# Attention with beacon keys, then a SwiGLU block: the hand-written order of the first quarter and of its loads written anew

## The chip, the cores and the metric

The kernel runs on one core of a Trainium2 chip. The metric is the device time of one execution in microseconds. A core has TensorE (PE, matrix products), VectorE (DVE), ScalarE (ACT), GpSimd (POOL), SyncE (SP, here only an issuer of DMAs) and 16 DMA engines; each engine works through its own instructions in order, and semaphores tie them together.

## What is computed

Attention over 8 batches of 8 heads, 576 tokens and head size 64, with 16 extra "beacon" keys in front that every token sees; then a gated feed-forward block on the 4608 tokens.

```python
k_all = np.concatenate([beacon_k, k], axis=2)
v_all = np.concatenate([beacon_v, v], axis=2)
scores = scale * np.matmul(q, k_all.transpose(0, 1, 3, 2))
scores = np.where(causal, -1000000000.0, scores)      # beacon columns are never masked
a = np.exp(scores - scores.max(-1, keepdims=True))
a /= a.sum(-1, keepdims=True) + 1e-09
x = np.matmul(a, v_all).transpose(0, 2, 1, 3).reshape(4608, 512)
g = x @ w_gate                                         # 512 -> 1536
return (g / (1 + np.exp(-g)) * (x @ w_val)) @ w_out    # 1536 -> 512
```

## The kernel before

All inputs come in as float32 and are turned into bfloat16 on the way, by DMAs that GpSimd issues (`rows`, `runs`, `w_load`, `load_wo`). A load takes one of eight DMA semaphores in turn, so the issue of a load waits for the landing of the load eight places earlier, and everything behind it on GpSimd waits too.

The work of one batch goes in four pairs of heads. Keys and queries have to be turned (head size onto the partitions). For batches 0 to 2 TensorE does that: `turn` (letter T in the plan below) writes `t_ps` in PSUM, and `turned_copy` brings it to `kT` and `qT`, on VectorE (K, Q) or on ScalarE (k, q). For batches 1 and 2 a pair's rows are first put side by side in SBUF by `pair_up`, on VectorE (g) or on GpSimd (f; 128x1152 elements into `side`). Later batches are turned by DMAs (t). The scores of a pair come in four units A to D (`scores`, S, or s where TensorE also adds the causal mask with two small products); `exponent` (E) is ScalarE's exp into `p`; `mask` sets masked elements to zero, on VectorE (D, a product with `ramp`) or on GpSimd (M, an affine select). `pv` (P and p, the two heads of a pair) multiplies with the values, `normalize` (R) on VectorE divides. The result is turned into `xT`, for batch 0 by TensorE (J, X), from batch 1 on by DMAs (V).

The feed-forward block goes over chunks of 512 tokens and 12 tiles of 128 hidden columns: `gate_value` (G, H; `gv_ps`) needs `wg` and `wv`, then tanh on ScalarE (a) and two products on VectorE (1, 2) give `hT`, and `project` (F; `o_ps`) multiplies with `wo`. Chunk 0 is cut: hidden tiles 0 to 5 are done for 240 tokens (units 0 to 5), then for 272 (units 6 to 11), then tiles 6 to 11 for all 512. The weights of `wg` and `wv` come in five parts each (g0 to g4, u0 to u4; parts 0, 1 and 2 hold hidden tile 0, tiles 1 and 2, and tiles 3 to 5), `wo` in two (o0, o1). K1, Q1, K2, Q2 are the keys and queries of batches 1 and 2, K0.0, Q0.0, K0.4, Q0.4 the later part of batch 0's for heads 0 to 3 and 4 to 7, v0.0 to v0.5 the beacon rows and five pieces of the values of batch 0, b1 and b2 beacon keys.

What every engine does, and in which order, is written out by hand: the string `plan` has one letter for each step, read from front to end, and each engine gets its steps in that order. Loads stand in the plan as L (free) or l (issued only after TensorE has done the step two before), and `order_of_loads` names which load each of them is. PSUM is cut into four slots of two banks (`take`, `give`): a step that takes a slot waits, on TensorE, for the step that gave that slot back. A letter h orders a filler, a product of 256 columns whose result nobody reads; it is put out at the next step that takes a slot for scores or values, and it writes into that slot:

```python
def keep_warm(ps):
    while heat:
        heat.pop()
        wide = ident[:, None, :].to_broadcast([P, 2, P])
        nc.tensor.matmul(ps[:, 0, 0 : 2 * P], lhsT=ident[:], rhs=wide, start=True, stop=True)
```

Of the kernel before, what the change touches and what calls it, by code (L numbers as in the profile page):

```python
# [84 lines left out]
def kernel(  # L85
# [731 lines left out]
    plan = """
    0LhbTqLLhhWKehTQsLTLEKLsqLkELhhSLTcQsKELKEsLssQEshsEhDELshEEELLhLTQZkNZsNSPpJEEILsJPLLERIpSXLDRP
    pSyEGXRHELDSyLDGaELGH1H2aaXD1Lf2Py1pGGLH2GRaXHlylH12aaGGH112a2HG1G2Haa1HaTq2lgGl1H2k1GaS21l2HSEa
    lsElGS12ETHgKQGEaS12lEHlTDa1GSqH2glDkESfaGslE1H2ElSEMDlTGMSQaKEHSMM12aGEs1HEa2T1qPpMllkDPfllSpRE  # L820
    2sRfsPDpSEEFEFFSFRDFFlSElSPEMpTFFlFERkFSfFFlqDSSFFFlEDFDEFSFTEFDFFFSQVlEkEFFDDFFOSEOllFFTtFqKFDl
    MSFESFFFFElSSMDlFElPplPlpERsFDFRFFFEFStlFFEGSGHtFDHDEaGMF1FFaH12POlOpaPp2RlG1GlRHtal2G1HHGVa21ll
    l2ltGHal1G2lGHHa1aatlt21tGH1H2lattF2aGFH112FF2FFGSaEFlHt1GFFaHa2Gltl1t2GtlH12latH12Fa12FFGGtDHSl
    tlaE1FHFFaG2lSFHtl12allF12GFElMFllFHaSG1FEFHaGFFolMHl2l1G2aSOF1H2FaE1FtFG2sHFEaFslF1FDFlSE2FDFED
    FSESlPpFFFRlDFFFlStFESSDFFEFFsEDFOPEpMPEOpSFFlFRMStRFEFEFSsFEMEFFDFFPplFSFFFFFlFRDSSEFEtFtSFDFFF
    FFEEFlVFFsoOElFFSFtFFDFtSMPEDEtSFElpSDRFFMFFtlMPtESSFEEpRFttFFGFDDSEGHFGa12HHlla1aG21FHl2aGlFHl1
    a2GSHD1ool2aDtPlEGM1ltp2HRlla1GtlSlGH2alEGHG1l2FaM1HHF2a1GFa2HS1FF2FSFFaEFSFEF12lFSPEFpDMFEFSlSR
    FFlEFFtSFttEFFDFSFVFFESEtFFFMsMDEFFFDFEsOFSFFolPttDEFDFSpFFEMFsESFRFFFEFFtFPMEGGOtHoSEtaplHRPtla
    11Gpt2HD2tGMRaGSt1HH2tGEa1al2G1HSa2GEH1a2GttHGa12SHH1a2MEG1GaM2DSHHES12FaEFFFFF1FDla2FFPSF1FE2Fp
    RFFSFFSEFSFESFFFFVEFSFFFFDDFEFFEFFDSoFPFFMlFpFEStlFERFFFFFSSDoEPMFFEFFFDDOMGpoRSElPHGa1S2pHEaR1G  # L830
    2sHlGGEDaHaD12GG1Ha2H12aG1Ha2HaGG12S1EHlHGa2a1D2MSH1FEl2GSMFa1H2EMPaFDF1FSF2EDFFFpSFEFFsRFFFSFFF
    SEFPEEFFSFpERFFSFFFMDVFMSFFDEEPFFDSoFFFFpFFFFEFDOFSPRFDFSpEGFFFEGRGDDFHaO1oHH2aa12P1GpRHGGH2VaGH
    a1a12HG2Ga1H122HGa1Ga2G1HHH2aa1a21G21GH2aG12HaHGFFFF1a2FFGF1H2aHaGF1H2FaF1GF2F1GHHFFFaa2FF12G1GH
    aFFFFH12F2FFFFFFaG1FHFFoFaFoFF212GGFHaFF1FHFF2FFaFGFFFFOHoG12GHHFaa12GFaFFF1FFF21FHF2GGFFaHFaFF1
    FFF12FHa2FG1GFHF2HFaF1FoaFFoFFFFFG2FF1FFHFaF1FGFF2HGFFFaFF12FH2FFaFFFFF1FFFFF2oFFFFFFFFFFFFOFFFF
    FFFOFoFFFFFFFFFFFOoFFFFFFOo
    """
# [42 lines left out]
```

## Time and profile before

| | us |
|---|---|
| median of 3 runs | 363.26 (363.25 to 364.06) |
| the profiled execution | 364.0 |
| its span in the trace | 362.0 |
| TensorE busy in the span | 353.9 (98%) |
| VectorE, ScalarE, GpSimd busy | 223.6, 189.0, 123.8 |
| mean granted share of TensorE's clock | 0.995 |

The span begins with the first instruction of the core and ends with the last one; 2.0 us of the profiled execution lie around it. Times in rows of the trace count from the start of the span. A row of the timeline merges equal instructions that follow each other ("x6"); in brackets behind a row stand the idle time of its engine just before it and what ended that. A matmul's row is longer than the distance to the next one, since matmuls overlap in the array.

### The profile page before, as it was taken

Reading aid. Unit: us, or ns where it says so; the run is one execution under the profiler, and the core shown is the slowest. Engines: PE = TensorE matmul, PEld = TensorE weight load, DVE = VectorE, ACT = ScalarE, POOL = GpSimd, SP = SyncE. Lnnn points to the kernel's source line nnn. Section 1 sums busy time; section 2 is a strip of 40 time slices with the busy share of each in tenths; the row PEclk is TensorE's granted clock in tenths of the full one; section 3 lists DMA queues with packets and bytes.
Section 4 is the critical chain, followed back from the end, with each engine's and each line's share of the span. In section 5 each row is a group of like instructions: output and inputs, shape, how many; then the busy total and the mean of one; then the engine's idle time right before and its main releaser. Section 6 shows DMA issues by size and latency. Waiting matters only on the chain.

```text
span 362.0 us, 11854 instructions
## 1 busy us (share of the span) xinstructions
PE 353.9 (98%) x5150; PEld 200.7 (55%) x5150; DVE 223.6 (62%) x437; ACT 189.0 (52%) x286; POOL 123.8 (34%) x185
## 2 busy tenths in 40 slices
PE   7899999999999999999999999999999999999996
PEld 4677566654444566544565556545655554455554
DVE  5577987667766753497518763777467764464341
ACT  4966989822425677543864466546633332331311
POOL 8935489936337544375423013112000000000000
PEclk9899999999999999999999999999999999999999
DMA  8999999999999999999999829602422000110113
GB/s 120 166 204 203 186 194 139 173 176 155 140 153 113 133 137 119 161 115 170 139 120 170 111 28 138 95 0 20 107 78 67 2 2 0 61 58 3 61 60 116
DMA packets 146132, 39.74 MB, mean 110 GB/s; under 512 B 131488, under 2 KB 141728, under 8 KB 146080
## 3 DMA queue, kind: packets, MB, share of 16 engines
q0 software_dynamic: 97424, 19.00, 73.4%
q1 hardware_dynamic: 48368, 19.76, 26.3%
q8 instruction: 40, 0.66, 0.8%
q10 hardware_dynamic: 288, 0.23, 0.2%
q14 instruction: 12, 0.10, 0.1%
HBM read 38.27 MB, written 9.44 MB: 132 GB/s over the span
## 4 chain that ended last, share of the span: by engine, by line
PE 84%; DMA 8%; POOL 4%; issue 3%; ACT 1%; POOLq 0%
PE gv_ps L173 46%; PE o_ps L173 26%; PE s_ps L173 5%; DMA wv<-in_moe_w_val_dram 4%; PE pv_ps L173 4%; PE pv_ps L505 3%; DMA wg<-in_moe_w_gate_dram 2%; DMA qk<-in_q_dram 2%; POOL qk L215 1%; POOL vb L225 1%; ACT p L414 0%; POOL wv L254 0%; POOL p L427 0%; POOL wo L258 0%; PE t_ps L171 0%
## 5 line engine op out<-in xcount | busy, mean ns | idle before, releaser
L173 PE MATMUL gv_ps<-xT,wv 64*128 64x512 bf16 (+2 forms) x912 | 203.2, 365 | 0.6 <-DMA wv<-in_moe_w_val_dram 0.6
L173 PE MATMUL gv_ps<-xT,wg 64*128 64x512 bf16 (+2 forms) x912 | 203.0, 365 | 0.1
L591 ACT ACTIVATE th<-gv_ps 128x512 f32<-128x512 f32 (+2 forms) x114 | 65.4, 575 | 118.0 <-PE gv_ps L173 117.6
L414 ACT ACTIVATE p<-s_ps 128x832 bf16<-128x832 f32 (+2 forms) x127 | 104.6, 869 | 34.4 <-PE s_ps L173 28.7
L173 PE MATMUL o_ps<-wo,hT 64*128 64x512 bf16 (+2 forms) x912 | 116.0, 365 | 0.4 <-ACT p L414 0.4
L596 DVE SCALAR_TENSOR_TENSOR u<-th,gv_ps 128x512 f32<-128x512 f32 (+2 forms) x114 | 74.7, 656 | 66.4 <-ACT th L591 65.7
L173 PEld LDWEIGHTS <-wg 64*128 64x128 bf16 x912 | 82.4, 94 | 45.7 <-PE gv_ps L173 2.4
L173 PEld LDWEIGHTS <-wv 64*128 64x128 bf16 x912 | 81.7, 94 | 40.7 <-DMA wv<-in_moe_w_val_dram 0.7
L603 DVE SCALAR_TENSOR_TENSOR hT<-gv_ps,u 128x512 bf16<-128x512 f32 (+2 forms) x114 | 74.7, 661 | 3.0
L173 PEld LDWEIGHTS <-hT 64*128 64x128 bf16 x912 | 43.4, 94 | 32.8 <-DVE hT L603 0.7
L225 POOL DMA_DIRECT2D vb<-in_v_dram x40 | 33.9, 851 | 63.0 <-PE s_ps L173 25.3
L173 PE MATMUL s_ps<-qT,kT 64*128 64x336 bf16 (+3 forms) x512 | 43.5, 254 | 1.4 <-ACT kT L262 0.8
L173 PEld LDWEIGHTS <-kT 64*128 64x128 bf16 x512 | 23.8, 94 | 22.6 <-issue 1.4
L423 DVE TENSOR_TENSOR p<-p,ramp 128x256 bf16<-128x256 bf16 (+2 forms) x84 | 23.9, 315 | 10.0 <-ACT p L414 9.8
L225 POOL DMA_DIRECT2D qk<-in_q_dram x25 | 21.2, 851 | 25.5 <-DMA qT<-qk 5.8
L534 DVE TENSOR_TENSOR x<-pv_ps,rec 128x640 bf16<-128x640 f32 (+1 forms) x32 | 25.3, 791 | 1.2
L533 DVE RECIPROCAL rec<-pv_ps 128x10 f32<-128x10 f32 (+1 forms) x32 | 6.8, 213 | 28.8 <-PE pv_ps L173 22.8
L225 POOL DMA_DIRECT2D qk<-in_k_dram x25 | 21.2, 851 | 5.7 <-PE gv_ps L173 4.4
L427 POOL TENSOR_SCALAR_AFFINE_SELECT p<-p 128x256 bf16<-128x256 bf16 (+2 forms) x46 | 17.5, 402 | 13.6 <-ACT p L414 13.3
L263 DVE COPY o_sb<-o_ps 128x512 f32<-128x512 f32 (+2 forms) x18 | 11.6, 657 | 16.5 <-PE o_ps L173 16.5
L173 PEld LDWEIGHTS <-p 64*128 64x128 bf16 x960 | 18.7, 94 | 4.5 <-PE pv_ps L173 0.2
L173 PE MATMUL pv_ps<-vb,p 64*128 64x65 bf16 x960 | 19.9, 189 | 0.0
(63 smaller groups left out, 142.8 us busy)
## 6 DMA issues: line engine op xcount, KB each, us to landing
out_dram<-o_sb SPq DMA_DIRECT2D x34, 256.0 KB, 3.6
vb<-in_v_dram POOLq DMA_DIRECT2D x24, 128.0 KB, 5.8
...
```

What stands on the lines that cost most here:

```text
L173: ins = nc.tensor.matmul(o, lhsT=l, rhs=r, start=start, stop=stop)
L225: return nc.gpsimd.dma_start(dst[p0 : p0 + n, c, :, 0:D], src[b, :, r : r + n, :].rearrange("h j d -> j h d"))
L263: return eng.tensor_copy(o, i)
L414: nc.scalar.activation(p_of(b, m, u == "A")[:, :, c0 : c0 + w], ps[:, :, 0:w], ACT.Exp, scale=0.125)
L423: nc.vector.tensor_tensor(out=ap, in0=ap, in1=upper[:, None, d : d + w].to_broadcast([P, 2, w]), op=ALU.mult)
L427: nc.gpsimd.affine_select(out=ap, in_=ap, compare_op=ALU.is_ge, fill=0.0, base=d, pattern=[[0, 2], [1, w]], channel_multiplier=-1,)
L505: ins = nc.tensor.matmul(o_ps[:, side, 68 * c : 68 * c + D + 1], lhsT=pt[n % NPT][:, side, col : col + P], rhs=vb[b % 2][:, t, 2 * m + sid ...
L533: nc.vector.reciprocal(rec[:, :, c0:NKT], o[:, :, :, D : D + 1])
L534: nc.vector.tensor_tensor(out=xs[b][:, c0:NKT, P * m : P * m + P].rearrange("p c (h d) -> p h c d", d=D), in0=o[:, :, :, 0:D], in1=rec[:, ...
L591: nc.scalar.activation(th[:, 0:w], gvs[n][:, 0, 0:w], ACT.Tanh, scale=0.5)
L596: nc.vector.scalar_tensor_tensor(out=u[:, 0:w], in0=ths[n][:, 0:w], scalar=1.0, in1=gvs[n][:, 0, 0:w], op0=ALU.add, op1=ALU.mult)
L603: nc.vector.scalar_tensor_tensor(out=hTs[j][:, f, c0:c1], in0=gvs.pop(n)[:, 1, 0 : c1 - c0], scalar=0.5, in1=ths.pop(n)[:, 0 : c1 - c0], o ...
```

## The change

Only the two strings are edited. In `plan`, the first 448 letters become 466; the 1307 letters behind them are the same. Up to that place each step occurs as often as before; what differs is the order, the engine of some steps, and the fillers:

| step, up to the common part | before | after |
|---|---|---|
| fillers (h) | 10 | 28 |
| masks on VectorE (D) / on GpSimd (M) | 22 / 9 | 10 / 21 |
| pairs put side by side on VectorE (g) / on GpSimd (f) | 3 / 5 | 0 / 8 |
| key copies on VectorE (K) / on ScalarE (k) | 7 / 6 | 6 / 7 |
| query copies on VectorE (Q) / on ScalarE (q) | 7 / 7 | 11 / 3 |
| batch 0's beacon copy | ScalarE (e) | VectorE (A) |
| later copies of `xT` (y / Y), of the output (O / o) | 4 / 0, 2 / 0 | 2 / 2, 1 / 1 |

The plan's second line shows how the values' steps of batch 0's pair 3 stand to unit 3 of the feed-forward block (the fourth G): before `...Py1pGG...` (P, p, then G3 and G4), now `...hPGap12a12G...` (P, G3, p, G4). The place where the common part begins is `POlOpaPp2RlG1G`, the values of batch 2, pairs 2 and 3.

The core of the diff:

```diff
     order_of_loads = """
-    K0.0 Q0.0 v0.2 Q0.4 K0.4 v0.1 v0.0 v0.3 v0.4 v0.5 g1 u0 g0 u1 g2 u2 K1 Q1 b1 u3 g3 g4 u4 Q2 v1.5 K2 v1.3
-    v1.2 v1.0 v1.1 v1.4 b2 o0 o1 v2.2 k3.0 v2.1 q3.2 v2.5 k3.5 v2.4 v2.3 v2.0 q3.4 q3.0 q4.2 k4.0 v3.3 k3.1 q4.0
+    Q0.0 K0.0 v0.0 K0.4 Q0.4 v0.2 v0.4 v0.1 v0.3 v0.5 u0 g1 g0 u1 u2 g2 K1 Q1 b1 u3 g3 b2 g4 u4 v1.0 Q2 K2 v1.1
+    v1.5 v1.3 v1.4 v1.2 o0 o1 q3.0 v2.2 q3.2 v2.1 v2.3 v2.0 v2.4 v2.5 k3.1 k3.5 k3.0 q3.4 k3.2 v3.3 q4.0 k4.2
...
     plan = """
-    0LhbTqLLhhWKehTQsLTLEKLsqLkELhhSLTcQsKELKEsLssQEshsEhDELshEEELLhLTQZkNZsNSPpJEEILsJPLLERIpSXLDRP
+    0TqTbQkLLWkAhhhshhhsTEQkhhhShsLETQEDLLkhhsLhsLLLLELETKLhsEQLELshhhsQhhhZEhhsKscEZNSEPNELLpEsPLpR
...
```

On ScalarE at the start, batch 0's copies out of `t_ps` (`qT_105`, `kT_107`) stand between the exps of the first units (`p_109`, `p_110`, `p_111` are the three buffers of `p`):

```order
 L262 ACTIVATE qT_105<-t_ps 128x256
-L262 ACTIVATE kT_107<-t_ps 128x4x16
-L414 ACTIVATE p_109<-s_ps 128x2x368
-L262 ACTIVATE qT_105<-t_ps 128x2x256
+L262 ACTIVATE kT_107<-t_ps 128x256 x2
+L414 ACTIVATE p_109<-s_ps 128x2x368
 L262 ACTIVATE kT_107<-t_ps 128x2x256
 L414 ACTIVATE p_110<-s_ps 128x2x368
 L414 ACTIVATE p_111<-s_ps 128x2x368
+L262 ACTIVATE kT_107<-t_ps 128x320
```

Three early key copies have come to ScalarE, the wide query copy and the beacon copy have left it.

Nine exps further on, still on ScalarE, the last key copy of batch 0 stood in the row of exps:

```order
 L414 ACTIVATE p_110<-s_ps 128x2x464
 L414 ACTIVATE p_110<-s_ps 128x2x416
-L262 ACTIVATE kT_107<-t_ps 128x2x320
 L414 ACTIVATE p_111<-s_ps 128x2x416
 L414 ACTIVATE p_111<-s_ps 128x2x464
```

It is now on VectorE, and the nine exps from batch 0's unit B of pair 0 on follow each other.

On GpSimd before, around the loads of `wo`: `qk_102` and `vb_103` are loads for batches 3 and 2, `side` is a pair of batch 2, the affine selects are masks of batch 1:

```order
L248 DMA beacons_100<-in_beacon_k_dram 16x8x64
L258 DMA wo<-in_moe_w_out_dram 128x6x512 x2
L263 COPY side<-qk_101 128x1152
L225 DMA vb_103<-in_v_dram 128x8x64
L225 DMA qk_102<-in_beacon_k_dram 16x8x64
L427 AFFINE_SELECT p_110<-p_110 128x2x128
L225 DMA vb_103<-in_v_dram 112x8x64
L427 AFFINE_SELECT p_111<-p_111 128x2x80
L427 AFFINE_SELECT p_111<-p_111 128x2x128
L427 AFFINE_SELECT p_109<-p_109 128x2x112
```

The same place now:

```order
L258 DMA wo<-in_moe_w_out_dram 128x6x512
L427 AFFINE_SELECT p_110<-p_110 128x2x112
L427 AFFINE_SELECT p_110<-p_110 128x2x128
L263 COPY side<-qk_102 128x1152
L427 AFFINE_SELECT p_110<-p_110 128x2x128
L427 AFFINE_SELECT p_111<-p_111 128x2x112
L427 AFFINE_SELECT p_111<-p_111 128x2x128
L258 DMA wo<-in_moe_w_out_dram 128x6x512
L263 COPY side<-qk_101 128x1152
L225 DMA qk_102<-in_q_dram 128x8x64
L225 DMA vb_103<-in_v_dram 128x8x64
L427 AFFINE_SELECT p_111<-p_111 128x2x128
```

Masks of batch 1, pairs 0 and 1, have moved ahead of the second load of `wo` and of batch 2's first pair; the beacon load b2 has left this place for one behind g3.

## Rows read from the trace of the kernel before

**Rows 1.** The page: busy time by engine.
```profile
PE 353.9 (98%) x5150; PEld 200.7 (55%) x5150; DVE 223.6 (62%) x437; ACT 189.0 (52%) x286; POOL 123.8 (34%) x185
```

**Rows 2.** Windows of 4 us: busy PE, PEld, DVE, ACT, POOL; clock, DMA, GB/s.
```profile
12.00:16.00 4.00, 4.00 (x98) 2.86 (x93) 1.16 (x4) 4.00 (x6) 3.40 (x6) 0.63 2.04 160
...
28.00:32.00 4.00, 4.00 (x71) 3.41 (x73) 3.18 (x9) 1.99 (x6) 0.37 (x1) 1.00 1.32 201
```

**Rows 3.** Timeline of ScalarE, batch 0: start, length, what.
```profile
11.47 4.81 ACT L414 ACTIVATE p<-s_ps 128x832 bf16<-128x832 f32 x6
16.11 0.77 ACT L262 ACTIVATE kT<-t_ps 128x640 bf16<-128x640 bf16 x1
17.23 2.46 ACT L414 ACTIVATE p<-s_ps 128x832 bf16<-128x832 f32 x3 [0.35 <-PE s_ps L173]
```

**Rows 4.** The chain of waits, 12 to 58 us: start, length, what.
```profile
15.16 7.66 DMA wg<-in_moe_w_gate_dram
...
23.11 15.64 DMA wv<-in_moe_w_val_dram
```

**Rows 5.** Timeline of TensorE around the fourth unit of the feed-forward block.
```profile
24.53 0.89 PE L505 MATMUL pv_ps<-vb,p 128*128 128x65 bf16 x24
25.37 0.26 PE L173 MATMUL gv_ps<-xT,wg 64*128 64x240 bf16 x1
26.18 0.27 PE L173 MATMUL gv_ps<-xT,wv 64*128 64x240 bf16 x1 [0.56 <-DMA wv<-in_moe_w_val_dram]
```

**Rows 6.** Timeline of TensorE, fillers of the start.
```profile
5.96 0.61 PE L187 MATMUL s_ps<-ident 128*128 128x256 bf16 x4
...
7.95 0.39 PE L187 MATMUL s_ps<-ident 128*128 128x256 bf16 x2
```

**Rows 7.** Timeline of TensorE behind that place, to the common part.
```profile
33.56 0.63 PE L173 MATMUL gv_ps<-xT,wg 64*128 64x272 bf16 x2
...
35.55 0.83 PE L173 MATMUL s_ps<-qT,kT 64*128 64x336 bf16 x8
...
49.92 1.47 PE L505 MATMUL pv_ps<-vb,p 128*128 128x65 bf16 x39
51.78 0.35 PE L505 MATMUL pv_ps<-vb,p 128*128 128x65 bf16 x6 [0.39 <-POOL p L427]
...
55.38 0.82 PE L173 MATMUL o_ps<-wo,hT 64*128 64x512 bf16 x6 [0.38 <-ACT p L414]
...
57.32 1.08 PE L505 MATMUL pv_ps<-vb,p 128*128 128x65 bf16 x30
...
78.00 1.99 PE L505 MATMUL pv_ps<-vb,p 128*128 128x65 bf16 x60
```

**Rows 8.** Timeline of GpSimd.
```profile
13.66 0.74 POOL L254 DMA_DIRECT2D wg<-in_moe_w_gate_dram  x1 [0.24 <-DMA qk<-in_k_dram]
...
46.40 0.82 POOL L258 DMA_DIRECT2D wo<-in_moe_w_out_dram  x1 [2.29 <-DMA qk<-in_k_dram]
47.22 1.16 POOL L263 COPY side<-qk 128x1152 bf16<-128x1152 bf16 x1
...
50.91 1.78 POOL L427 TENSOR_SCALAR_AFFINE_SELECT p<-p 128x160 bf16<-128x160 bf16 x5
```

**Rows 9.** Timeline of VectorE: a mask alone, and one while GpSimd copies (third row, GpSimd).
```profile
40.61 0.47 DVE L423 TENSOR_TENSOR p<-p,ramp 128x224 bf16<-128x224 bf16 x2
...
53.99 1.75 DVE L423 TENSOR_TENSOR p<-p,ramp 128x224 bf16<-128x224 bf16 x2
...
54.24 1.16 POOL L263 COPY side<-qk 128x1152 bf16<-128x1152 bf16 x1
```

**Rows 10.** Groups of instructions by shape, 0 to 80 us: count, busy us, mean ns.
```profile
L534 DVE TENSOR_TENSOR x<-pv_ps,rec 128x640 bf16<-128x640 f32 x7 | 5.8, 824 | 0.2
L603 DVE SCALAR_TENSOR_TENSOR hT<-gv_ps,u 128x512 bf16<-128x512 f32 x8 | 5.5, 688 | 0.2
...
L263 DVE COPY kT<-t_ps 128x576 bf16<-128x576 bf16 x3 | 2.2, 750 | 0.0
```

More of the change, by code (lines that the diff above doesn't have):

```diff
@@ L734 @@
     order_of_loads = """
-    K0.0 Q0.0 v0.2 Q0.4 K0.4 v0.1 v0.0 v0.3 v0.4 v0.5 g1 u0 g0 u1 g2 u2 K1 Q1 b1 u3 g3 g4 u4 Q2 v1.5 K2 v1.3
-    v1.2 v1.0 v1.1 v1.4 b2 o0 o1 v2.2 k3.0 v2.1 q3.2 v2.5 k3.5 v2.4 v2.3 v2.0 q3.4 q3.0 q4.2 k4.0 v3.3 k3.1 q4.0
-    k3.4 k3.2 q3.1 v3.0 k4.2 q3.3 k4.3 v3.5 q4.4 k3.3 v3.4 v3.2 k4.5 k4.1 q4.3 q4.1 v4.1 v4.5 v4.3 v4.0 k4.4
+    Q0.0 K0.0 v0.0 K0.4 Q0.4 v0.2 v0.4 v0.1 v0.3 v0.5 u0 g1 g0 u1 u2 g2 K1 Q1 b1 u3 g3 b2 g4 u4 v1.0 Q2 K2 v1.1
+    v1.5 v1.3 v1.4 v1.2 o0 o1 q3.0 v2.2 q3.2 v2.1 v2.3 v2.0 v2.4 v2.5 k3.1 k3.5 k3.0 q3.4 k3.2 v3.3 q4.0 k4.2
+    q4.2 k4.0 q3.1 q3.3 v3.0 k3.4 k4.3 v3.5 q4.4 k3.3 v3.4 v3.2 k4.5 k4.1 q4.3 q4.1 v4.1 v4.5 v4.3 v4.0 k4.4
     v3.1 v4.2 q6.1 k5.0 q5.1 q5.4 k5.3 k5.5 k6.0 k5.2 k5.1 q5.0 k6.2 q5.3 v4.4 k6.1 q6.0 q6.2 k6.5 q5.2 v5.2
@@ L817 @@
     plan = """
-    0LhbTqLLhhWKehTQsLTLEKLsqLkELhhSLTcQsKELKEsLssQEshsEhDELshEEELLhLTQZkNZsNSPpJEEILsJPLLERIpSXLDRP
[L819 to L836, printed above, removed]
+    0TqTbQkLLWkAhhhshhhsTEQkhhhShsLETQEDLLkhhsLhsLLLLELETKLhsEQLELshhhsQhhhZEhhsKscEZNSEPNELLpEsPLpR
+    SXEJyRIJIMPXEYpLRhShSLLLlEGGDHEGMXHLa1YHM2hPGap12a12GRHGLXla1yHf2aHaL1212lGGHHfGaa1G1l2HaHGa2T1H
@@ new lines @@
+    2Qlk1Gl2al1SEfHlhhhST2aGEsk1Q2EHla1SMGSEHE2STDQGEKSaH1sEfaM2MGlDfESHE12a1SGllE2MSHEaTsGqK1T2MHEP
+    QSpDkllMsaEP12ERsEpSRfPSlDpEESMFFFfTFRFElSllKqPSEpFMSFEFFFESlERFFTfVFFMlQkSSMEEFFFMMSEMFFFFFFFFF
+    DMTSlFOlotFEQlKFFFFSFESPpESMFFMEllRFPplRDsltlFEDlFSFFFESEDGMGHaFFFFHFGlF1ltM2Fla1HPOlOpaPp2RlG1G
+    lRHtal2G1HHGVa21lll2ltGHal1G2lGHHa1aatlt21tGH1H2lattF2aGFH112FF2FFGSaEFlHt1GFFaHa2Gltl1t2GtlH12l
+    atH12Fa12FFGGtDHSltlaE1FHFFaG2lSFHtl12allF12GFElMFllFHaSG1FEFHaGFFolMHl2l1G2aSOF1H2FaE1FtFG2sHFE
@@ new lines @@
+    aFslF1FDFlSE2FDFEDFSESlPpFFFRlDFFFlStFESSDFFEFFsEDFOPEpMPEOpSFFlFRMStRFEFEFSsFEMEFFDFFPplFSFFFFF
+    lFRDSSEFEtFtSFDFFFFFEEFlVFFsoOElFFSFtFFDFtSMPEDEtSFElpSDRFFMFFtlMPtESSFEEpRFttFFGFDDSEGHFGa12HHl
+    la1aG21FHl2aGlFHl1a2GSHD1ool2aDtPlEGM1ltp2HRlla1GtlSlGH2alEGHG1l2FaM1HHF2a1GFa2HS1FF2FSFFaEFSFEF
+    12lFSPEFpDMFEFSlSRFFlEFFtSFttEFFDFSFVFFESEtFFFMsMDEFFFDFEsOFSFFolPttDEFDFSpFFEMFsESFRFFFEFFtFPME
+    GGOtHoSEtaplHRPtla11Gpt2HD2tGMRaGSt1HH2tGEa1al2G1HSa2GEH1a2GttHGa12SHH1a2MEG1GaM2DSHHES12FaEFFFF
@@ new lines @@
+    F1FDla2FFPSF1FE2FpRFFSFFSEFSFESFFFFVEFSFFFFDDFEFFEFFDSoFPFFMlFpFEStlFERFFFFFSSDoEPMFFEFFFDDOMGpo
+    RSElPHGa1S2pHEaR1G2sHlGGEDaHaD12GG1Ha2H12aG1Ha2HaGG12S1EHlHGa2a1D2MSH1FEl2GSMFa1H2EMPaFDF1FSF2ED
+    FFFpSFEFFsRFFFSFFFSEFPEEFFSFpERFFSFFFMDVFMSFFDEEPFFDSoFFFFpFFFFEFDOFSPRFDFSpEGFFFEGRGDDFHaO1oHH2
+    aa12P1GpRHGGH2VaGHa1a12HG2Ga1H122HGa1Ga2G1HHH2aa1a21G21GH2aG12HaHGFFFF1a2FFGF1H2aHaGF1H2FaF1GF2F
+    1GHHFFFaa2FF12G1GHaFFFFH12F2FFFFFFaG1FHFFoFaFoFF212GGFHaFF1FHFF2FFaFGFFFFOHoG12GHHFaa12GFaFFF1FF
@@ L837 @@
+    F21FHF2GGFFaHFaFF1FFF12FHa2FG1GFHF2HFaF1FoaFFoFFFFFG2FF1FFHFaF1FGFF2HGFFFaFF12FH2FFaFFFFF1FFFFF2
+    oFFFFFFFFFFFFOFFFFFFFOFoFFFFFFFFFFFOoFFFFFFOo
     """
```

## Prediction

> **What bounds the kernel now.** The page comes first: TensorE is busy 98% of the span, no other engine over 62% [rows 1]. An edit that leaves TensorE's products alone can only take away time in which it waits, and all 8 us of idle time are spread over the span. Both strings change nothing behind the place where the common part of the plan begins, which TensorE reaches at 78.00 [rows 7]. So the question is when it gets there.
>
> Next come the windows and the timelines of the first 78 us. There are three stretches. **The first, to about 20 us, is ScalarE's**: from 11.47 its exps follow each other without a gap, six in 4.81 us (0.80 each), then a key copy of 0.77, a wait of 0.35, three more exps [rows 3], and the window from 12 to 16 shows it busy for 4.00 of 4.00 us [rows 2]. TensorE's clock stands at 0.63 in that window, so partly at the lower level, behind a stretch in which it had little to do; ScalarE sets the pace there, so it costs little.
>
> **The second ends at a landing.** At 25.37 TensorE begins the fourth unit of the feed-forward block (G3), the first that reads the third weight parts g2 and u2, and stands until 26.18 for the DMA of `wv` [rows 5]. This DMA isn't late because it was issued late. The chain shows a transfer issued at 15.16 that takes 7.66 us and one issued at 23.11 that takes 15.64, to 38.75 [rows 4]: they stand behind other transfers, and the DMA engines move about 200 GB/s from 28 to 32 us with a busy share over 1 [rows 2]. What lands when is decided by the bytes ahead of it.
>
> **The third, 26 to 78 us**, is TensorE at work with small holes. Matched with rows of the same shape, I find five [rows 7]: at 33.56 a pair of products spaces out to 0.63 where 0.39 is usual (0.24); at 35.55 eight products for scores take 0.83 where two groups would take 0.55 (0.28); from 49.92 to 52.07 45 products of the values take 2.14, where 30 take 1.01 to the next start (57.32), hence 1.52 (0.6); 0.2 between there and 54; 0.4 to 0.5 before 55.38, for an exp. That is about 1.8 us, and all that is to be had behind the landing. The hole at 49.92 is GpSimd's: the masks of batch 1 (five pieces, 1.78 us from 50.91) stand behind the second load of `wo`, which waited 2.29 us for a landing, and behind a 1.16 us copy [rows 8].
>
> **The change, part by part.**
>
> *Before the landing.* (a) ScalarE loses the 0.77 us key copy and the 0.35 us wait between its exps [rows 3], and gets three early key copies while it waits for scores anyway; its ninth exp from 11.47 on ends about 1.1 us earlier, about 18.6. For that the second half of batch 0's keys and queries must be turned earlier. Now their loads go ahead of v0.2; before, the later of the two was in only when the load issued at 13.66 could go (its wait is for that DMA) [rows 8]; a small beacon load now stands in front instead of v0.2's 128 KB, 0.7 us earlier at the 160 GB/s of that window [rows 2]. (b) The output of the values and the turns of `x` follow; working the queues of TensorE, ScalarE and VectorE by hand with these durations I get G3 reached at about 25.0. (c) The 18 more fillers cost 0.11 us each at the full clock (four take 0.61, two 0.39 [rows 6]), 0.21 at the half one: 2.0 to 3.8 us of TensorE. Fifteen of them lie before G3, where TensorE waits for exps and for slots; that cover, ScalarE's exps, holds as long as G3 is reached before its weights.
> The sum of this part is nothing: whether G3 is reached at 25.4 or 25.0, it begins at the landing. g2 and u2 have changed places, but the later of the two has the same bytes ahead of it, so 26.2 (between 25.2, if the 0.7 us of earlier issue counts in full, and 26.6).
>
> *At the landing.* P, p, G3 has become P, G3, p. The second half of the values of pair 3, half of the 24 products that take 0.84 to the next start [rows 5], used to be done before 26.18 and now comes behind: +0.4. Three of the new fillers stand behind the landing too, in front of scores of batch 1: +0.3 at the full clock, less where a slot is awaited; bounds 0 and 0.6.
>
> *Behind the landing.* The side-by-side copies go ahead of where they are needed, and G10 stands before the first turn, so the holes at 33.56 and 35.55 close: -0.5. The masks of batch 1, pairs 0 and 1, now run before GpSimd waits for the load of `wo`, and the values of pairs 0 to 2 are set between scores: by hand their masks are there 0.5 to 4 us before they are read. The hole of 0.6 and the one of 0.2 close. What comes late instead is VectorE: in that stretch it has to do two units of 0.69 + 0.69, three normalizations of 0.82 + 0.22, and turned copies of 0.75 [rows 10], some 8 us in a row, and each slot that the values take is given back by one of these. I find TensorE waiting about 0.25 twice there; the wait before the first `project` stays, but two units of scores are done ahead of it. So of the 1.8 us I take 1.2 as gained; bounds 0.3 and 1.8.
>
> *GpSimd's load.* Three more side-by-side copies at 1.16 and twelve more masks at 0.36 to 0.8 (one or two pieces [rows 8]) are about 9 us more before 78. From 28 to 32 it was busy for 0.37 of 4 us [rows 2], and behind 46 us the copies and masks of batch 2 stand 5 us or more before their readers. Costed at nothing; it would decide from some 5 us of lateness on.
>
> *One port, two engines.* A mask of two pieces takes VectorE 0.47 alone, 1.75 while GpSimd copies [rows 9]. The change leaves VectorE 10 masks and gives GpSimd all copies. The Trainium skill (SBUF — State Buffer, Who interferes with whom) says that a VectorE instruction with two SBUF inputs and a GpSimd instruction that reads SBUF lock each other out for a whole instruction; the row agrees, and by that rule more copies on GpSimd speak against the change: by an estimate from it, if each of the five copies from 42 us on met a VectorE mask, 5 x 1.28 = 6.4 us of VectorE and, at the share of the next sentence, 1.5 of TensorE, and the sum below would be +0.7. By the order I see one such meeting that matters (a mask of batch 1's pair 3 beside batch 2's second or third pair): 1.75 - 0.47 = 1.3 us of VectorE [rows 9], of which some 0.3 reaches TensorE; it is in the bounds above.
>
> **The sum.** +0.4 + 0.3 - 1.2 = -0.5 us, with ends +0.7 (0.4 + 0.6 - 0.3) and -1.4 (0.4 + 0 - 1.8). The durations are those of the profiled execution (364.0, span 362.0); it lies 0.7 above the median of 363.26, so the difference is taken from the median: **362.7 us**.
>
> **The rivals.** *The landing moves* (faster). If g2 and u2 land 0.8 to 1.0 earlier because their issue is 0.7 earlier, G3 begins at about 25.2, the wait of 0.56 goes, and all later landings with it: -0.5 - 0.9 = -1.4, about 361.8; with all five holes closed, 361.2. For it: the window 12 to 16 moves 160 GB/s, not 200 [rows 2]. Against it: loads of many small rows are in flight then, and the queue is never empty.
>
> *G3 is missed* (slower). The start is one chain: the fillers wait for a slot and then stand before the scores. If they run at the lower clock, or if the turns now in front of unit D wait for their loads until 13.4 as before [rows 8], ScalarE starves, and TensorE reaches G3 behind its weights. It decides from 1.2 us on (25.0 against 26.2). The price is everything beyond: with 15 fillers at 0.21 (3.2 us) not hidden at all, 3.2 - 1.2 = 2.0, less the 0.5: about 364.8.
>
> *The order does not do what it says* (no change). The holes close but VectorE's row behind 48 us opens as many: +0.4 + 0.3 - 0.7 = 0: 363.3.
>
> **How the numbers follow.** A measurement here can tell about 0.3% (1.1 us) from no change. Forecast 362.7: 0.46. No change, 363.3: 0.14. Both are within the 0.3%: 0.60. The landing moves: 0.27, just beyond it. G3 is missed: 0.13. The range reaches from 361.4 (most of the faster rival) to 364.5 (the near half of the slower one).
>
> **What would show it.** In the changed trace: nine exps on ScalarE from about 11.5 without a copy between them, the last ending before 19; TensorE waiting longer than 0.56 for `wv` or `wg` at G3 and going on at 26 to 26.4; no idle time for GpSimd's masks near 50; the first `project` near 55; the values of batch 2, pairs 2 and 3, at about 77.5 instead of 78.00. Wrong would be a G3 without a wait, a granted clock under 1 behind 16 us, or a GpSimd mask or copy that TensorE waits for behind 50 us.

## The result

The changed kernel takes **367.43 us** (median of 4 runs, 367.11 to 368.24) against 363.38 for the kernel before in the same session: a ratio of 1.0113, 95% interval 1.0096 to 1.013. It is slower by 4.1 us, where 362.7 was forecast and a range up to 364.5. In a later session the same kernel took 365.34 (364.24 to 367.33) against 363.83, ratio 1.0051 (1.0031 to 1.007). So there are two things to explain: a loss of 1.5 us (1.9 by the ratio) that is there in both sessions, and some 2 us more that come and go. One execution, the profiled one of after_masks_apart, ran at a low clock throughout and is left out. Each profile below is that of one execution, so the stretches within it are compared, and the medians stand beside them.

The page of the changed kernel, busy time by engine, answers to [rows 1]. TensorE has 4.5 us more, and its share is still 98%:

```profile
PE 358.4 (98%) x5168; PEld 203.9 (56%) x5168; DVE 220.2 (60%) x424; ACT 187.2 (51%) x281; POOL 132.5 (36%) x203
```

The windows of the changed kernel, with the columns of [rows 2]:

```profile
12.00:16.00 4.00, 2.74 (x72) 1.84 (x69) 1.96 (x5) 2.10 (x4) 3.02 (x5) 0.70 2.16 161
16.00:20.00 4.00, 4.00 (x46) 2.51 (x44) 2.49 (x9) 2.45 (x3) 2.12 (x3) 0.50 1.47 183
...
28.00:32.00 4.00, 4.00 (x77) 3.11 (x76) 3.19 (x9) 1.08 (x3) 1.18 (x3) 1.00 1.31 202
```

From 12 to 16 us ScalarE is busy for 2.10 of 4 us, where [rows 2] had 4.00. From 16 to 20 TensorE's granted clock is 0.50, the lower of its two levels (1.2 GHz instead of 2.4).

ScalarE in the same stretch, which answers to [rows 3]: two exps, a pause of 1.90, two, one, a pause of 1.46. There is no row of nine.

```profile
12.28 1.71 ACT L414 ACTIVATE p<-s_ps 128x832 bf16<-128x832 f32 x2
15.89 1.62 ACT L414 ACTIVATE p<-s_ps 128x832 bf16<-128x832 f32 x2 [1.90 <-PE s_ps L173]
17.66 0.94 ACT L414 ACTIVATE p<-s_ps 128x928 bf16<-128x928 f32 x1 [0.15 <-PE s_ps L173]
20.07 3.28 ACT L414 ACTIVATE p<-s_ps 128x832 bf16<-128x832 f32 x4 [1.46 <-PE s_ps L173]
```

What ScalarE waits for stands on TensorE. Its timeline in the changed kernel shows the turn of batch 0's heads 0 to 3 (the first row), the turn of heads 4 to 7 (the next two), a group of fillers, and then the place of [rows 5] and of the last row of [rows 7]:

```profile
10.71 0.51 PE L171 MATMUL t_ps<-ident,qk 64*64 64x64 bf16 x40 [0.45 <-DMA qk<-in_k_dram]
...
12.73 0.21 PE L171 MATMUL t_ps<-ident,qk 64*64 64x64 bf16 x1
14.21 0.74 PE L171 MATMUL t_ps<-ident,qk 64*64 64x64 bf16 x39 [1.26 <-DMA qk<-in_q_dram]
...
16.20 0.82 PE L187 MATMUL s_ps<-ident 128*128 128x256 bf16 x3
...
29.18 0.53 PE L505 MATMUL pv_ps<-vb,p 128*128 128x65 bf16 x12
29.64 0.27 PE L173 MATMUL gv_ps<-xT,wg 64*128 64x240 bf16 x1
...
30.15 0.53 PE L505 MATMUL pv_ps<-vb,p 128*128 128x65 bf16 x12
...
54.22 0.63 PE L505 MATMUL pv_ps<-vb,p 128*128 128x65 bf16 x15
...
56.24 0.61 PE L505 MATMUL pv_ps<-vb,p 128*128 128x65 bf16 x15 [0.25 <-ACT p L414]
...
82.39 1.78 PE L505 MATMUL pv_ps<-vb,p 128*128 128x65 bf16 x53
```

The turn of heads 4 to 7 begins at 12.73 and stands until 14.21 for a load of queries, in front of the scores that ScalarE needs next. G3 begins at 29.64, waiting for nothing. The chain of waits names the load (it is Q0.4, issued behind v0.0 and K0.4):

```profile
6.70 7.47 DMA qk<-in_q_dram
14.16 0.04 issue
14.21 0.74 PE t_ps L171 x32
14.95 0.33 PE s_ps L187
```

**The 4.5 us of the two spans (366.5 and 362.0) add up from four pieces.** The first turn got its load 1.05 later (10.71 against 9.66; over all traces that load lands at 9.6 to 10.8 in the new order and at 9.3 to 10.8 in the old one, so this is a difference between executions). From there to G3 it took 18.93 us against 16.52 (to 26.18 in [rows 5], where the products go on): 2.41. From G3 to the values of batch 2's pairs 2 and 3 it took 52.75 (29.64 to 82.39) against 51.82 (26.18 to 78.00): 0.93. Behind that, 284.1 against 284.0. So the third piece, forecast as a gain of 0.5, is a loss of 0.93, and the second, forecast as nothing, is the large one.

### The profile page after: what moved, and what is told of

The parts are those of the page before. It is cut to its first block, busy times and chain, and to the rows that moved or that the text cites. A ratio compares the mean times of both kernels' runs of the same rounds, so it can differ in the third digit from the quotient of the medians.

```text
span 366.5 us, 11889 instructions
## 1 busy us (share of the span) xinstructions
PE 358.4 (98%) x5168; PEld 203.9 (56%) x5168; DVE 220.2 (60%) x424; ACT 187.2 (51%) x281; POOL 132.5 (36%) x203
## 4 chain that ended last, share of the span: by engine, by line
PE 93%; DMA 2%; DVE 2%; POOL 1%; ACT 1%; issue 0%; POOLq 0%
PE gv_ps L173 50%; PE o_ps L173 26%; PE s_ps L173 7%; PE pv_ps L173 4%; PE pv_ps L505 4%; DMA qk<-in_q_dram 2%; POOL qk L215 1%; PE t_ps L171 1%; PE s_ps L187 1%; DVE hT L603 1%; DVE u L596 0%; DVE qT L263 0%; PE pvf_ps L446 0%; ACT th L591 0%; PE xt_ps L548 0%
## 5 line engine op out<-in xcount | busy, mean ns | idle before, releaser
L427 POOL TENSOR_SCALAR_AFFINE_SELECT p<-p 128x256 bf16<-128x256 bf16 (+2 forms) x61 | 23.1, 403 | 17.1 <-ACT p L414 17.0
L423 DVE TENSOR_TENSOR p<-p,ramp 128x256 bf16<-128x256 bf16 (+2 forms) x69 | 17.7, 290 | 7.0 <-ACT p L414 6.7
## 6 DMA issues: line engine op xcount, KB each, us to landing
qk<-in_k_dram POOLq DMA_DIRECT2D x2, 576.0 KB, 10.8
```

What stands on the lines that cost most here:

```text
L423: nc.vector.tensor_tensor(out=ap, in0=ap, in1=upper[:, None, d : d + w].to_broadcast([P, 2, w]), op=ALU.mult)
L427: nc.gpsimd.affine_select(out=ap, in_=ap, compare_op=ALU.is_ge, fill=0.0, base=d, pattern=[[0, 2], [1, w]], channel_multiplier=-1,)
```

## The experiments

### Old and new halves put together

One kernel has the new order up to G3 and the old one behind it, one the reverse (the two are joined just behind the third unit, so a few steps in front of G3 go with the later half). Against the change:

```diff
 early_new
-...GGDHEGMXHLa1YHM2hPGap12a12GR...
+...GGDHEGMaH1H2aaXD1Lf2Py1pGGLH2GR...
 late_new
-...GGDHEGMXHLa1YHM2hPGap12a12GR...
+...SyLDGaELGXHL1YHM2hPGap12a12GR...
```

> The new order up to the third unit of the feed-forward block, with the new loads up to g3 and b2, and the order of before behind it. If the loss of 4 us lies in the start (turn of the second half of batch 0, clock, fillers, landings: TensorE reached the first feed-forward unit at 26.14 instead of 21.27 and the fourth at about 29.7 instead of 26.18), this loses 3 to 4 us: 366.4 to 367.4. If the start only moves a wait that the third stretch pays anyway, it stays within 1 us of before: 362.4 to 364.4.

> The order of before up to that place, the new order and the new loads behind it. The prediction's third stretch said -0.5 us (holes of 1.2 us closed against 0.7 added): 362.3 to 363.2. If instead VectorE's row of normalizations, copies and products bounds that stretch (the changed trace lost 0.9 us more between the fourth unit and the common part), it loses 0.5 to 1.5: 363.9 to 364.9.

Measured, against 363.71 before: early_new 364.29 (363.04 to 368.30, ratio 1.0034, interval 1.0001 to 1.0068), late_new 365.29 (365.06 to 365.41, ratio 1.0043, 1.0028 to 1.0058). Eight of the ten times of early_new lie between 363.0 and 364.9, two at 368.2 and 368.3. In its profile the turn of heads 4 to 7 had its load at 13.12, and G3 began at 26.47. In late_new G3 to the values of batch 2 took 52.66, close to the 52.75 of the change.

So the half behind G3 costs about 0.9 us in both traces; the half before G3 costs little in most executions and over 4 us in some. Two things stay open. The two slow times of early_new have a mean granted clock of 0.990 and 0.989, like the first profile of the changed kernel (0.989), but neither was traced. And late_new is 1.6 us behind by its median where its trace shows 0.84 behind G3; its first loads were in at 10.81, against 9.62 to 10.00 in the kernel before, and how much of the rest comes from that is not shown.

### Two edits of the early half

The turn of heads 4 to 7 (T) put behind two units of scores and a query copy; and nine of the early fillers (h) taken out:

```diff
 after_turn_late
-...LLLLELETKLhsEQLELshhhsQhhhZEhh...
+...LLLLELEKLhsEQLELshhhsTQhhhZEhh...
 after_fewer_fillers
-...LLLLELETKLhsEQLELshhhsQhhhZEhhsKscE...
+...LLLLELETKLsEQLELssQZEsKscE...
```

> The changed kernel with one step moved: the turn of batch 0's second half and its first copy stand behind unit C of pair 1 instead of before unit D of pair 0. If TensorE's stop at this turn (1.3 us at 12.9, ScalarE without exps from 14.0 to 15.9) and the lower clock that follows it make the loss, three exps run under the wait and 2 to 3.5 us come back: 364.0 to 365.5. If the fillers behind the turn (nine at 0.21 to 0.25 us) are the cause, it gains under 1 us: over 366.4. If the late landing itself (14.16) decides, because everything behind the turn starts from it, 0.5 to 1.5 us come back.

> The changed kernel without the nine fillers between that turn and the values of pair 0. If they are in the way (they took 0.33 + 0.75 + 0.61 + 0.55 us at the lower clock in the trace), 2.2 us come back: about 365.2. If TensorE waits there anyway, or if the lower clock lasts longer without them, nothing or a loss: 367.0 to 368.5.

Measured: after_turn_late 366.28 (365.92 to 366.73, ratio 1.0071, 1.0054 to 1.0088), after_fewer_fillers 365.24 (364.28 to 367.76, ratio 1.0055, 1.0033 to 1.0078). With the turn behind the scores the clock stayed at the full level, but the copies and constants that follow the turn on VectorE then held up a unit of scores (TensorE waits 1.30 us for VectorE at 18.73), and G3 came 17.26 behind the landing of the later of Q0.0 and K0.0. So the turn's place is no gain by itself: the 366.28 is above the 364.0 to 365.5 of that theory, and it falls in the range of the third case (0.5 to 1.5 us back) by luck, since the later load was in at 12.48 here and the turn at 14.37 waited for nothing. The 365.24 without nine fillers is what was forecast if they are in the way, but the changed kernel with all of them took 365.34 in a later session, so that they cost anything is not shown. The kernel with fewer fillers is the one in which the forecast's picture of ScalarE came true; its timeline:

```profile
11.91 7.46 ACT L414 ACTIVATE p<-s_ps 128x832 bf16<-128x832 f32 x9
20.26 0.45 ACT L262 ACTIVATE xT<-xt_ps 128x336 bf16<-128x336 bf16 x1 [0.89 <-PE xt_ps L548]
```

Nine exps without a gap, ending at 19.37, and yet G3 began at 26.05, which is 16.46 behind that landing (9.59); the order before needs 15.75 (below). Closing ScalarE's gap does not bring G3 forward: behind its ninth exp ScalarE waits 0.89 us for a turn of `x` on TensorE.

### The kernel before, once more

> The kernel before once more, to see whether its wait for the weights at G3 is there in another execution. Theory (the landing of u2 at 26.14 was that execution's; other executions have the later of g2 and u2 at 24.2 to 25.4): G3 begins 15.7 to 16.1 behind the landing of the second of K0.0 and Q0.0 and waits for no weights. Rival (the landing of u2 bounds G3): a wait of 0.3 or more for the DMA of wv, G3 going on at 25.9 to 26.3.

One run, 363.51. TensorE's timeline in it:

```profile
9.94 0.51 PE L171 MATMUL t_ps<-ident,qk 64*64 64x64 bf16 x39 [0.28 <-DMA qk<-in_q_dram]
14.25 0.51 PE L171 MATMUL t_ps<-ident,qk 64*64 64x64 bf16 x40
...
24.80 0.89 PE L505 MATMUL pv_ps<-vb,p 128*128 128x65 bf16 x24
25.64 0.26 PE L173 MATMUL gv_ps<-xT,wg 64*128 64x240 bf16 x1
...
77.46 1.99 PE L505 MATMUL pv_ps<-vb,p 128*128 128x65 bf16 x60
```

G3 begins at 25.64 and goes on without a wait; u2 had landed at 24.27. From G3 to the values of batch 2 it is 51.82 again, and from the landing of Q0.0 (9.89) to G3 15.75, as in the first profile (9.62 and 25.37). **The wait of [rows 5], on which the forecast's cover rested, belonged to one execution.** In all traces but that one the later of g2 and u2 lands between 24.2 and 25.4. And the turn of heads 4 to 7 stands at 14.25 behind the scores; its later load landed at 13.49, so it has a margin of 0.8.

### The suspected load issued two places later

```diff
-    Q0.0 K0.0 v0.0 K0.4 Q0.4 v0.2 v0.4 v0.1 ...
+    Q0.0 K0.0 v0.0 K0.4 v0.2 v0.4 Q0.4 v0.1 ...
```

The changed kernel itself was run again too; nothing is edited in it.

> The changed kernel once more, to see whether its early stretch comes out alike in another execution. Theory (the turn of batch 0's second half stands in front of the scores and waits for loads whose landing differs from run to run, 11.5 to 14.2 us; the lower clock that follows makes the fillers dear): 366.5 to 368 us, G3 between 27.5 and 30 without a wait for weights, the stretch from G3 to the values of batch 2's pairs 2 and 3 unchanged at 52.75. Rival (the time of 367.4 was owed to that one session): 365.3 or less, like the kernel without nine of the fillers.

> The changed kernel with one load issued two places later (Q0.4, the later queries of heads 4 to 7, behind two pieces of the values). Theory (in the execution at 367.4 us that load landed at 14.2, where other executions have it at 11.5 to 13.1; the turn that reads it stands in front of TensorE's scores, ScalarE's exps run dry, the granted clock falls to its lower level and the fillers take twice as long): it lands at 14.0 to 15.5, the turn waits for it, the first unit of the feed-forward block begins 14 to 16 us behind the landing of the second of Q0.0 and K0.0 (12.5 to 13 otherwise), 366.8 to 368.5 us in every execution. Rival (the slow early stretch has its cause elsewhere): 365.0 to 365.6, like the changed kernel in the second session.

The kernel with the late load takes 367.84 (367.24 to 370.20, ratio 1.0118, 1.0068 to 1.0167), the changed kernel 365.34. TensorE's turn and the windows in the kernel with the late load:

```profile
12.24 0.21 PE L171 MATMUL t_ps<-ident,qk 64*64 64x64 bf16 x1
14.32 0.74 PE L171 MATMUL t_ps<-ident,qk 64*64 64x64 bf16 x39 [1.86 <-DMA qk<-in_q_dram]
```

```profile
12.00:16.00 4.00, 2.13 (x59) 1.43 (x57) 1.36 (x4) 1.50 (x2) 3.90 (x6) 0.77 2.08 168
16.00:20.00 4.00, 4.00 (x68) 2.64 (x64) 2.86 (x10) 3.44 (x5) 0.87 (x2) 0.80 1.49 195
```

The load lands at 14.27 and the picture of the changed kernel's first profile is back: the wait at the turn, ScalarE at 1.50 of 4 us, a granted clock under 1 behind it, G3 18.29 behind the landing of K0.0 (18.98 in the first profile). Where the load lands between 11.5 and 13.1 (four traces with the new order of this turn and of the loads) that distance is 15.97 to 16.60. **So a landing that comes 1 to 3 us later costs 1.7 to 3.0 us, and it explains the profiled execution of the session at 367.4.** The other three of that session (367.11 to 367.59, mean granted clock 0.993 to 0.997) were not traced. The first unit of the block began 14.79 behind the landing, as expected (14 to 16).

The price has two parts, the wait itself (1.26 and 1.86 idle) and what comes behind it at the lower clock. The trace of early_new helps to part them: there the same turn also waits, 1.02 us, but the granted clock stays at 1.00 (from 12 to 16 us too), and G3 comes only 16.60 behind the landing.

```profile
13.16 0.51 PE L171 MATMUL t_ps<-ident,qk 64*64 64x64 bf16 x39 [1.02 <-DMA qk<-in_q_dram]
```

```profile
16.00:20.00 4.00, 3.84 (x97) 2.93 (x93) 2.97 (x12) 3.96 (x5) 2.05 (x4) 1.00 1.51 195
```

From the end of that turn to the first unit of the feed-forward block, with the same steps between them, it is 9.08 us there (13.67 to 22.75) and 9.07 in after_again and after_masks_apart_2, both at the full clock. It is 9.91 in the kernel with the late load (15.06 to 24.97) and 11.19 in the first profile of the changed one (14.95 to 26.14). So 2.1 us of the first profile's price lie behind the turn, in the stretch with the lower clock, and 0.8 of the other's, where more of the price is the wait. That the clock alone makes the longer stretch is not shown: ScalarE runs out of scores at the same time, and one of the four times of the kernel with the late load is 367.24 at a mean granted clock of 1.000.

### The old order of loads

The changed plan with the whole old string of loads.

> The changed kernel with the loads in the old order. Theory (the turn of batch 0's second half stands in front of TensorE's scores and waits for its loads; the later of the two lands at 13.4 to 13.6 in the old order, at 11.5 to 14.2 in the new one): TensorE waits at that turn until 13.5, the first unit of the feed-forward block begins 13.0 to 14 us behind the landing of the second of K0.0 and Q0.0, the median is 365.8 to 367 us. Rival (the wait at that turn is covered by ScalarE's exps): 365.3 us, like the changed kernel.

Measured: 370.92 (369.86 to 371.71, ratio 1.018, 1.0151 to 1.0209), much more than expected, and for another reason. The first unit of the block began 13.26 behind the landing, within the expected range, but TensorE then stood in the values of batch 2 (first row). On GpSimd (the other rows) the mask it waited for came behind loads of batches 3 and 4, which had waited for a transpose by DMA:

```profile
83.39 0.93 PE L505 MATMUL pv_ps<-vb,p 128*128 128x65 bf16 x25 [2.93 <-POOL p L427]
```

```profile
76.77 0.83 POOL L225 DMA_DIRECT2D qk<-in_k_dram  x1 [5.94 <-DMA kT<-qk]
...
82.86 0.48 POOL L427 TENSOR_SCALAR_AFFINE_SELECT p<-p 128x256 bf16<-128x256 bf16 x1
```

That wait is part of the 4.8 us that the kernel loses behind the start of these values (288.9 to the end of the span, 284.1 in the changed kernel); the granted clock was 0.57 from 84 to 88 us. The two strings belong together: one letter in `plan` is another load when the other string changes, and what stands behind it on GpSimd waits with it.

### Masks beside copies

In the profile of after_again G3 to the values of batch 2 took 54.70, not 52.75. Its timelines of VectorE, GpSimd and TensorE show where most of the 2 us are:

```profile
41.78 1.42 DVE L423 TENSOR_TENSOR p<-p,ramp 128x160 bf16<-128x160 bf16 x1
...
45.76 1.89 DVE L423 TENSOR_TENSOR p<-p,ramp 128x160 bf16<-128x160 bf16 x1
...
48.28 0.69 DVE L603 SCALAR_TENSOR_TENSOR hT<-gv_ps,u 128x512 bf16<-128x512 f32 x1
```

```profile
41.23 0.77 POOL L427 TENSOR_SCALAR_AFFINE_SELECT p<-p 128x224 bf16<-128x224 bf16 x2
41.92 1.17 POOL L263 COPY side<-qk 128x1152 bf16<-128x1152 bf16 x1
...
45.55 0.84 POOL L258 DMA_DIRECT2D wo<-in_moe_w_out_dram  x1 [1.40 <-PE s_ps L173]
46.38 1.16 POOL L263 COPY side<-qk 128x1152 bf16<-128x1152 bf16 x1
```

```profile
49.02 0.38 PE L173 MATMUL s_ps<-qT,kT 64*128 64x336 bf16 x4 [0.88 <-DVE hT L603]
```

Two masks of VectorE meet two copies of GpSimd and take 1.42 and 1.89 us; the first begins beside a mask of GpSimd (until 42.00), the second beside the issue of the second load of `wo`. In the first profile of the changed kernel they took 0.31 and 0.23. VectorE's products for the feed-forward block come late by that, and TensorE stands at three places, with rows spaced out by 0.53, 0.31 and 1.15. Laid beside the changed kernel's first profile, which has small holes of its own there, that is 1.5 us: from G3 to the first values of batch 1 it is 26.07 (26.78 to 52.85) against 24.58. The other 0.46 of the 1.95 stands elsewhere, in a wait within a group of values at 57.62 that the trace puts down to no engine; the kernel with the late load has it too, without a meeting. The edit puts these masks (D) on GpSimd (M):

```diff
-...SEHE2STDQGEKSaH1sEfaM2MGlDfESHE1...
+...SEHE2STMQGEKSaH1sEfaM2MGlMfESHE1...
```

> The changed kernel with the two masks of batch 1 that VectorE has between 41 and 47 us (pair 0's and pair 1's unit B) on GpSimd, behind each other with its copies instead of beside them. Theory (these masks of 160 columns take 1.42 and 1.89 us beside GpSimd's copy where they take 0.23 alone, and TensorE then waits about 2 us in all): G3 to the values of batch 2's pairs 2 and 3 is 52.6 to 52.9 in this execution and never 54.7, the median goes from 365.3 to between 363.6 and 364.6 us. Rival (the masks only meet the copies in the executions that the profile caught, or GpSimd's longer row is waited for): 365.0 to 365.6 us.

> The kernel with VectorE's two masks between 41 and 47 us on GpSimd once more, for a trace at the full clock. Theory (TensorE's waits of 0.53, 0.31 and 1.15 between 43 and 49 us come from these masks beside GpSimd's copies): no wait over 0.2 there, G3 to the values of batch 2's pairs 2 and 3 at 52.6 to 52.9. Rival (something else on GpSimd or VectorE is late there): 53.5 or more.

The first run gave a median of 365.16 (364.42 to 366.29), ratio 1.003 (1.0013 to 1.0047); the second is for a trace. In the second, 364.73, TensorE has no wait from 42 to 50, and G3 to the values of batch 2 takes 52.99 (25.97 to 78.96). The waits are gone, so the masks beside GpSimd's work were their cause. But the median moved by 0.2 only, where 0.7 to 1.7 was expected: the meeting happens in some executions. Of the ten times of after_again two are over 367, one of them the profiled one; of the nine here the highest is 366.29. That is in keeping with it, but too few to count a frequency. Of the ten traces with both masks on VectorE, three show one of over 1.2 us (after_again, after_fewer_fillers, late_fix_beacons).

### What the new order costs behind G3

Three edits on late_new: batch 1's and 2's first query copies back on ScalarE (beacons); the two halves of a pair's values joined (merge); and both together, with unit 3 behind all values of pair 3 and without four fillers (all). A fourth kernel has the merge, the moved unit and fillers, and the masks of the section above on GpSimd, but not the query copies.

```diff
 late_fix_beacons
-...Ga2T1H2Qlk1Gl2... ...MHEPQSpDkll...
+...Ga2T1H2qlk1Gl2... ...MHEPqSpDkll...
 late_fix_merge
-...MHEPQSpDkllMsaEP12ERsEpSRfPSlDpEESM...
+...MHEPpQSDkllMsaEPp12ERsESRfPpSlDEESM...
 late_fix_all, besides both; late_masks_merge, besides the merge and the masks
-...YHM2hPGap12a12GR... ...SEfHlhhhST2a...
+...YHM2PpGa12a12GR... ...SEfHlST2a...
```

> The old order up to G3, the new one behind it, with the two query copies in front of beacon copies (batch 1's and batch 2's first pair) back on ScalarE. Theory (ScalarE's beacon copy, and the tanh and exps queued behind it, wait for VectorE's query copy of the same turn): the two holes of 0.40 and 0.42 close, G3 to the values of batch 2's pairs 2 and 3 goes from 52.66 to about 51.9, 364.5 us against 365.3 of the same kernel without this edit. Rival (ScalarE, with 1.5 us more to do, delays tanh and exps by as much): 52.5 to 52.8, 365.3 us.

> The old order up to G3, the new one behind it, with the second half of each pair's values of batch 1 set directly behind the first half (four joins). Theory (a group of value products costs TensorE about 0.15 us beyond its products for 15 of them and 0.20 for 30, so each cut costs 0.10 us): G3 to the values of batch 2's pairs 2 and 3 goes from 52.66 to about 52.2, 364.9 us. Rival (the halves now wait for their masks or exps): 52.7 to 53.2, 365.3 to 365.8 us.

> The old order up to G3, the new one behind it, with both edits above, and with unit 3 of the feed-forward block again behind all values of batch 0's pair 3 and without the filler in front of it and the three in front of batch 1's unit B (0.8 us of work that had come behind G3). Theory (these three make up the difference to the forecast): G3 to the values of batch 2's pairs 2 and 3 at 50.7 to 51.0 against 51.82 before (counted from 26.18, where the weights are in), 362.3 to 363.2 us. Rival (other holes open in their place): 51.5 to 52, 363.5 to 364 us.

> The old order up to G3, the new one behind it, with these two masks on GpSimd, the halves of the values of batch 1 joined, unit 3 behind all values of pair 3, and without the four fillers behind G3. Theory (masks beside copies, cuts and added work behind G3 are what the new order lost): G3 to the values of batch 2's pairs 2 and 3 at 51.6 to 51.9, 363.8 to 364.2 us, no slower than before by more than 0.1%. Rival (what is left over is ScalarE's beacon copies, which wait for VectorE, with 0.5 to 1 us): 52.3, 364.6 us.

Measured: beacons 364.94 (ratio 1.0045, 1.0025 to 1.0065), merge 365.06 (1.0023, 1.0008 to 1.0037), all 364.64 (1.0024, 1.0011 to 1.0038), masks and merge 363.70 (0.9998, 0.9978 to 1.0018). G3 to the values of batch 2, against 52.66 without an edit: 55.08, 52.62, 52.06 and 51.76.

- *The query copies*: the theory fell. The changed kernel's timeline of ScalarE shows a beacon copy that waits for VectorE, with a tanh behind it; with the copy on ScalarE the hole at this turn stayed (0.42), and the one at batch 1's first turn grew from 0.40 to 0.69, since three copies in a row end later than two beside each other. (The 55.08 has two meetings of masks and copies in it, which cost TensorE 2.0 there; the 367.47 of that execution is not its median.)

```profile
54.75 0.22 ACT L262 ACTIVATE kT<-t_ps 128x64 bf16<-128x64 bf16 x1 [0.61 <-DVE qT L263]
54.87 0.59 ACT L591 ACTIVATE th<-gv_ps 128x512 f32<-128x512 f32 x1
```

- *The joins*: the rival held. Four cuts less give back 0.4, and a wait of 0.72 for an exp takes it, in front of the next pair's values:

```profile
50.48 1.08 PE L505 MATMUL pv_ps<-vb,p 128*128 128x65 bf16 x30
...
52.76 1.07 PE L505 MATMUL pv_ps<-vb,p 128*128 128x65 bf16 x30 [0.72 <-ACT p L414]
```

- *The work put behind G3*: 52.62 - 51.76 = 0.86 between merge and the fourth kernel, neither with a meeting of mask and copy in its trace. Laid side by side, 0.72 of it is there by 37 us: that is the second half of pair 3's values and the fillers. The other 0.14 comes around 55 us, where merge's values are spaced out more.
- *All together*: 52.06 and 364.64 are behind both the theory and the rival. Its stretch is 0.30 longer than the fourth kernel's, and the hole at batch 1's first turn, 0.29 longer with the query copies on ScalarE, accounts for that.

The fourth kernel came out as forecast and ties with the kernel before. So the new order behind G3, without the work moved there, is worth what the old one is.

### One part alone, on the kernel before

Three masks of batch 1 (M) ahead of the loads (l) from the second of `wo` on, two of them ahead of batch 2's first side-by-side copy (f) too:

```diff
-...qH2glDkESfaGslE1H2ElSEMDlTGMSQaKEHSMM12a...
+...qH2gDkESaGsE1H2ESEMDTGMfSQaKEHSMlllMl12a...
```

> The kernel before with one part of the change alone: three masks of batch 1 stand on GpSimd ahead of the second load of wo and of batch 2's first pair, instead of behind them. Theory (the hole of 0.65 at 49.92 is owed to these masks): it closes, 26.18 (or G3's start where that is later) to the values of batch 2's pairs 2 and 3 goes from 51.82 to about 51.2, 363.2 us against 363.8 before. Rival (pair 1's first half then waits for scores or a slot as long): 51.8, no difference.

Measured: **362.85** (361.94 to 364.58) against 363.59, ratio 0.9972, interval 0.9955 to 0.9989. GpSimd and TensorE in it, which answer to [rows 8] and [rows 7]:

```profile
43.91 0.69 POOL L427 TENSOR_SCALAR_AFFINE_SELECT p<-p 128x256 bf16<-128x256 bf16 x2
45.52 1.14 POOL L263 COPY side<-qk 128x1152 bf16<-128x1152 bf16 x1 [0.92 <-DMA qk<-in_k_dram]
46.61 0.41 POOL L427 TENSOR_SCALAR_AFFINE_SELECT p<-p 128x256 bf16<-128x256 bf16 x1
47.41 0.84 POOL L258 DMA_DIRECT2D wo<-in_moe_w_out_dram  x1 [0.39 <-PE s_ps L173]
```

```profile
49.59 1.53 PE L505 MATMUL pv_ps<-vb,p 128*128 128x65 bf16 x45
...
53.95 0.81 PE L173 MATMUL o_ps<-wo,hT 64*128 64x512 bf16 x6
...
76.55 1.99 PE L505 MATMUL pv_ps<-vb,p 128*128 128x65 bf16 x60
```

The 45 products run through, and the first `project` waits for no exp (0.38 in [rows 7], 0.90 in before_again). G3 to the values of batch 2 takes 50.79 (25.76 to 76.55) instead of 51.82: 1.03 gained, more than the 0.65 of the hole, since the wait behind it went too. The two are one loss that falls differently from one execution to the next: in before_again the 45 products take 1.69 to the next start instead of 2.14, so the hole is mostly closed there, and the first `project` waits longer (0.90), and G3 to the values of batch 2 is 51.82 in both. It is the fastest kernel here, ahead of both.

## Why the prediction was wrong

**"Whether G3 is reached at 25.4 or 25.0, it begins at the landing": this step failed, and with it the cover.** The wait of 0.56 stood in the one profile at hand, where u2 landed at 26.14. In before_again and every other trace the weights are there 0.7 us or more before G3. So the stretch before G3 is not covered; what it loses counts in full: 2.41 us in the first profile, where the forecast had nothing. Two of the forecast's own signs of being wrong are in that trace, a G3 without a wait and a granted clock under 1 behind 16 us.

**"I get G3 reached at about 25.0": too early.** From the landing of Q0.0 at 9.62 that is 15.4. Where the changed kernel's loads came early it took 15.97 to 16.46 (the last without nine fillers), and 15.75 in the order before. The nine exps came true in one kernel and did not help. Too small by 0.6 to 1.1.

**"The later of the two was in only when the load issued at 13.66 could go": read rightly, used wrongly.** The two loads were to land 0.7 earlier; they were issued 0.4 earlier (6.09 and 6.70 instead of 6.49 and 7.10), and an earlier issue was taken as an earlier landing. In the changed order the load landed anywhere from 11.5 to 14.2, and the turn had lost its place behind the scores that gave it 0.8 us of margin. The rival *G3 is missed* names what happened, the turn's wait, the lower clock, ScalarE without scores. Its chance (0.13) leaned on a cover that wasn't there, and its price on 15 fillers alone. Measured: 2.4 us from the first turn to G3 in the first profile, beside 0.93 behind G3.

**At the landing, +0.4 and +0.3: right.** 0.86 by difference, 0.72 of it by 37 us; forecast 0.7.

**Behind the landing, -1.2: failed.** The old holes at 33.56, 49.92 and 54 did close. New ones opened: 0.40 behind batch 1's first turn, 0.42 at 55.82 for an exp, and six more cuts between values and scores at about 0.11 each (two groups of 15 products take 0.56 each to the next start, one of 30 takes 1.01). 52.75 - 51.82 = 0.93 is the added work of 0.86 and next to nothing else. That is the rival *the order does not do what it says*, and about 0 in place of the 0.7 it allowed. TensorE waits there for the copies of a turn and for exps; that VectorE's row is the cause, as the rival had it, is not shown, since the query copies on ScalarE closed neither hole.

**"I see one such meeting that matters", some 0.3: too small.** In after_again two masks met copies, and both ended within 0.2 us of the copy's end. The Trainium skill (SBUF — State Buffer, Who interferes with whom) says that a VectorE instruction with two SBUF inputs and a reading one of GpSimd lock each other out for a whole instruction; the trace agrees, with these ends. They cost VectorE 2.85 us (1.42 + 1.89 - 2 x 0.23) and TensorE 1.5, so about half, where the forecast took a quarter. The forecast looked for meetings in one order of events, and which instructions meet depends on when loads land.

**Three more copies and twelve more masks on GpSimd, "costed at nothing": right as to lateness**; TensorE waits for no mask or copy of GpSimd behind 50 us in the changed kernel. What the copies cost where they meet VectorE's masks is the point above. And the best part of the change is the one this rests on: masks ahead of loads that wait.
